# Sliding-window attention with a SwiGLU block: half of the first tile's shifted values by DMA, earlier keys for tile 1, and the last output rows in two column halves

## The chip, the cores and the metric

The kernel runs on one core of one Trainium2 chip. The metric is the device time of one execution in microseconds (us): 337.42 us is the median of three runs before the change (337.41 to 337.79). The profile is of one execution with a span of 335.7 us; times inside it count from the start of that span. Engine names are those of the profile: PE is TensorE (matmuls; PEld are its weight loads), DVE is VectorE, ACT is ScalarE, POOL is GpSimd, SP is SyncE. ACTq, SPq and POOLq are the engines' issues of transfers.

## What is computed

Eight batches of 8 heads with 576 positions and 64 channels go through causal attention with a window of 64 positions; the heads are joined, and each of the 4608 rows of 512 channels goes through a SwiGLU block of width 1536.

```python
scores = scale * np.matmul(q, k.transpose(0, 1, 3, 2))
mask = (rel >= 0) & (rel < window)                       # rel = query position - key position
attn = softmax(np.where(mask, scores, -1e9))
x = np.matmul(attn, v).transpose(0, 2, 1, 3).reshape(B * S, H * D)
g = x @ w_gate
out = (g * sigmoid(g) * (x @ w_val)) @ w_out
```

Inputs and output are float32 in HBM; the kernel multiplies in bfloat16 and accumulates in float32.

## The kernel before

The rows are worked in nine tiles of 512. A tile is 512 positions of one batch; tile 7 (LAST) gathers the last 64 positions of all eight. The order of the instructions on every engine is written out by hand: each engine takes its instructions in program order, and waits in order.

**A tile** has three stages. In the first, for each of four head pairs u, `scores` (L201) multiplies keys and queries into PSUM, ScalarE takes the exponential (L233) and VectorE the mask (L235). `sums` adds up the weights with a matmul by ones (`totals`, L245), and ScalarE makes the reciprocal from Ln and Exp (L253, L256). `values` (L265) multiplies the weights with v, block by block of 64 positions: even blocks take their values from `v2`, odd blocks from `v1`. `v2` holds the same values as `v1`, shifted by 64 positions (`shift_v`, L150: the lower half of a block's partitions comes from the block before, the upper half is copied). VectorE scales the product into xT (L277). In the second stage, `gate_value` (L302) runs for twelve values of m: four matmuls into a gate bank and four into a value bank, ScalarE's Silu (L299), and VectorE's product into hT (L300). Each bank has two buffers. In the third stage, `project` (L339) multiplies four groups of 128 rows with wo, twelve matmuls each over c (L315), VectorE copies the result from PSUM (L322), and four transfers of 32 rows store it (L334). The projection of tile t-1 is interleaved with the attention of tile t.

**Tile 0 and the opening** are written out by hand (L351 to L485). q, k and half of v of tile 0 come by transfers of SyncE and ScalarE, the other half of v by GpSimd's (L430), which cast on the way. TensorE runs matmuls on a tile of ones without use (`keep_warm`, L366) while it has nothing to do; their number in each place is fixed. GpSimd then issues in one row the gate weights (L442 to L447), the queries of tile 1 (`load_qk(1)`), wo in three parts (L449 to L451) and v of tile 1. They go through one queue in that order. GpSimd's issues have a limited number of lanes, and each waits for an earlier load in its lane. VectorE fills v2 of tile 0 in four copies (L462, L463, lines L155 and L156 of `shift_v`), after the last key split of tile 0 (L177). Then TensorE runs six warm matmuls, values of pairs 0 and 1, totals of pair 2 (`log_of`), gate matmuls, and totals of pair 3 between them.

**Keys of tile 1** come as float32 by four ScalarE transfers, issued in the gate loop of tile 0 at m = 3 to 6 (L500), are cast and joined by ScalarE at m = 7 to 10 (L505), transposed by TensorE and split by VectorE at m = 8 to 11 (L506 to L510). VectorE turns the queries of tile 1 at m = 10, 11 and twice after the loop (`turn_q`, L186). Then come scores(1,0) and scores(1,1), half of two projections of tile 0 with wo's parts c = 0 to 5, scores of the other two pairs, and c = 6 to 11.

**The end**: after the gates of tile 8, L582 runs four projections with nothing else left. Their stores are issued by SyncE and ScalarE in turn.

Of the kernel before, what the change touches and what calls it, by code (L numbers as in the profile page):

```python
# [8 lines left out]
P = 128  # L9
FP32 = mybir.dt.float32  # L10
# [7 lines left out]
def kernel(  # L18
# [10 lines left out]
    nc = tc.nc  # L29
    S, D, H = 576, 64, 8  # L30
    NTOK, DFF, DM = 4608, 1536, 512
    NT = NTOK // 512
# [9 lines left out]
    fsb = ctx.enter_context(tc.tile_pool(name="fsb", bufs=3))  # L42
# [6 lines left out]
    wo = cst.tile([P, 12, DM], BF16, name="wo")  # L49
# [4 lines left out]
    ones = cst.tile([P, 512], BF16, name="ones")  # L54
# [15 lines left out]
    staged, queries, weights, inverse, xT, hT = {}, {}, {}, {}, {}, {}  # L70

    def load_runs(eng, dst, src, t, hs):
        eng.dma_start(
            dst.rearrange("r h e d -> r h (e d)"),
            src[batch(t), hs, 0:512].rearrange("h (r e) d -> r h (e d)", e=4),
        )
# [73 lines left out]
    def shift_v(t, copy, lo=0, hi=4):  # L150

        a, b = v1[t % 2], v2[t % 2]
        top = min(hi, 3)
        if top > lo:
            copy(b[64:128, lo + 1:top + 1], a[64:128, lo:top])  # L155
        copy(b[0:64, lo:hi], a[0:64, lo:hi])  # L156
# [14 lines left out]
    def transposes(tp, src):  # L171

        for e in range(4):
            nc.tensor.transpose(tp[:, P * e:P * e + P], src[:, e], identb[:])  # L174
# [7 lines left out]
    def turn_q(t, u):  # L182

        if u == 0:
            queries[t] = att.tile([P, 4, 512], BF16, name="qT", tag="qT")
        nc.vector.transpose(  # L186
            queries[t][:, u, :].rearrange("r (e x) -> r e x", e=16),
            staged[t][0][:, u].rearrange("r (e d) -> r e d", d=D)[:, :, 0:32],
        )
# [53 lines left out]
    def totals(t, u, d_ps):  # L243
        for h in range(2):
            nc.tensor.matmul(  # L245
                d_ps[64 * h:64 * h + 64], ones[:, 0:D], weights[t, u][:, h, :]
            )

    def room(n):
        return fsb.tile([P, 2, 512], FP32, name="r", tag="r", bufs=4)[:, 0:n]  # L250

    def log(r, d_ps):
        nc.scalar.activation(r, d_ps, AF.Ln)  # L253
# [11 lines left out]
    def values(t, u, o_ps):  # L265
        E = weights.pop((t, u))
        if u == 0:
            xT[t] = att.tile([P, 4, 512], BF16, name="xT", tag="xT")
        for m in range(8):
            for h in range(2):  # L270
                nc.tensor.matmul(  # L271
                    blocks(o_ps[64 * h:64 * h + 64], t, m, m + 1),
                    (v1, v2)[m // 4][t % 2][:, m % 4, 2 * u + h, :] if t == LAST
                    else (v2, v1)[m % 2][t % 2][:, m // 2, 2 * u + h, :],
                    blocks(E[:, h, :], t, m, m + 1),
                )
        nc.vector.tensor_mul(xT[t][:, u, :], o_ps[:], inverse.pop((t, u)))  # L277
# [5 lines left out]
    def gate_part(t, ms, tiles, c):  # L283
        for m, pair in zip(ms, tiles):
            for ps, w in zip(pair, (wg, wv)):
                nc.tensor.matmul(  # L286
                    ps[:], w[:, c, P * m:P * m + P], xT[t][:, c, :],
                    start=(c == 0), stop=(c == 3),
                )

    def gate_tiles():
        return [ps_f.tile([P, 512], FP32, name=x + "_ps", tag=x) for x in "gv"]

    def gate_end(t, m, pair):
        if m == 0:
            hT[t] = hpool.tile([P, 12, 512], BF16, name="hT", tag="hT")
        g_ps, v_ps = pair
        sg = fsb.tile([P, 512], FP32, name="sg", tag="sg")
        nc.scalar.activation(sg[:], g_ps[:], AF.Silu)  # L299
        nc.vector.tensor_mul(hT[t][:, m, :], sg[:], v_ps[:])  # L300

    def gate_value(t, m):  # L302
        pair = gate_tiles()
        for ps, w in zip(pair, (wg, wv)):
            for c in range(4):
                nc.tensor.matmul(  # L306
                    ps[:], w[:, c, P * m:P * m + P], xT[t][:, c, :],
                    start=(c == 0), stop=(c == 3),
                )
        gate_end(t, m, pair)  # L310

    def project_part(t, ss, tiles, cs):
        for c in cs:
            for s, o_ps in zip(ss, tiles):
                nc.tensor.matmul(  # L315
                    o_ps[:], hT[t][:, c, P * s:P * s + P], wo[:, c, :],
                    start=(c == 0), stop=(c == 11),
                )

    def project_end(t, s, o_ps):  # L320
        os_ = fsb.tile([P, 512], FP32, name="os_", tag="os_", bufs=3)
        nc.vector.tensor_copy(os_[:], o_ps[:])  # L322
        rows = out[S * batch(t):S * batch(t) + 512]
        if t < TURNED:
            nc.sync.dma_start(rows.rearrange("(r e) f -> e r f", e=4)[s], os_[:])
            return
        if t == LAST:
            rows = out.rearrange("(b s) f -> b s f", s=S)[:, 512:S]
            rows = rows.rearrange("b (r e) f -> e b r f", e=16)
        else:  # L330
            rows = rows.rearrange("(r e) f -> e r f", e=16)
        for i in range(4):
            eng = nc.scalar if t == NT - 1 and i % 2 else nc.sync
            eng.dma_start(rows[4 * s + i], os_[32 * i:32 * i + 32])  # L334

    def out_tile():
        return ps_f.tile([P, 512], FP32, name="o_ps", tag="g")

    def project(t, s):  # L339
        o_ps = out_tile()  # L340
        project_part(t, (s,), (o_ps,), range(12))
        project_end(t, s, o_ps)

    def set_exp():
        nc.scalar.preload_act_table_set("natural_log_exp_and_others")

# [6 lines left out]
    for u in range(4):  # L353
        hs = slice(2 * u, 2 * u + 2)
# [1 line left out]
        load_runs(nc.scalar if u < 2 else nc.sync, raw[1][:, hs], k, 0, hs)  # L356
    load_v(nc.sync, staged[0, "v"], 0, (0, 1))
    set_exp()
    nc.vector.memset(ones[:], 1.0)
    make_identity(nc, identb[:])  # L360
    nc.vector.memset(zero[:], 0.0)
    for i in range(2):
# [1 line left out]
    warm = ps_f.tile([P, 512], FP32, name="warm", tag="v")  # L364

    def keep_warm(n):  # L366
        for _ in range(n):
            nc.tensor.matmul(warm[0:D], ones[:, 0:D], ones[:])

    keep_warm(7)  # L370
    nc.gpsimd.memset(tri[:], 1.0)
    for a in range(2):
        half = tri[64 * a:64 * a + 64]
        nc.gpsimd.affine_select(
            out=half[:, 1 - a], in_=half[:, 1 - a], compare_op=ALU.is_ge, fill=0.0,
# [3 lines left out]
            out=half[:, a], in_=half[:, a], compare_op=ALU.is_ge, fill=0.0,  # L379
# [19 lines left out]
    on_v, on_p, on_a = nc.vector.tensor_copy, nc.gpsimd.tensor_copy, nc.scalar.copy  # L399
# [4 lines left out]
    def wide(name):  # L404
        return ps_a.tile([P, 2, 512], FP32, name=name, tag="a")

    def join(copy, dst, src):
        copy(dst.rearrange("r e (h d) -> r h e d", h=2), src)

    def one(name):  # L410
        return ps_a.tile([P, 2, 512], FP32, name=name, tag="a")[:, 0]
# [43 lines left out]
    d_ps, r = wide("d_ps"), room(2)  # L455
# [4 lines left out]
    invert(r)  # L460
    scores(0, 3)
    shift_v(0, on_v, 0, 2)  # L462
    shift_v(0, on_v, 2, 4)  # L463

    def log_of(u):
        d_ps = one("d_ps")
        totals(0, u, d_ps)
        inverse[0, u] = room(1)[:, 0]
        log(inverse[0, u], d_ps)

    keep_warm(6)
    for u in range(2):
        values(0, u, ps_f.tile([P, 512], FP32, name="ao_ps", tag="gv"[u])[:])
    log_of(2)
    pairs = [gate_tiles() for _ in range(2)]
    gate_part(0, (0,), pairs, 0)
    log_of(3)
    gate_part(0, (1,), pairs[1:], 0)
    for u in (2, 3):
        invert(inverse[0, u])  # L480
    values(0, 2, one("ao_ps"))
# [6 lines left out]
    for m in range(12):  # L488
        if m < 2:
            gate_end(0, m, pairs[m])  # L490
        else:
            gate_value(0, m)
        if m == 2:
            for i in range(4):
                nc.vector.tensor_copy(
                    mask[:, 0, :, i], tri[:].rearrange("r c (x e) -> r e c x", e=16)
                )
            nc.vector.memset(mask[64:128, 0, :, 0, 0, :], 0.0)
            nc.vector.tensor_copy(mask[:, 1], mask[:, 0])
        if 3 <= m < 7:  # L500
            hs = slice(2 * m - 6, 2 * m - 4)
            load_runs(nc.scalar, raw_k[:, hs], k, 1, hs)
        if 7 <= m < 11:
            u = m - 7
            join(on_a, keys[:, u], raw_k[:, 2 * u:2 * u + 2])  # L505
        if m >= 8:  # L506
            u = m - 8
            tp = ps_a.tile([P, 512], BF16, name="tp", tag="a")
            transposes(tp, keys[:, u])
            split_k(kT[1][:, u, :], tp[:])  # L510
        if m >= 10:
            turn_q(1, m - 10)
    turn_q(1, 2)
    turn_q(1, 3)

    set_exp()
# [27 lines left out]
    for t in range(1, NT):  # L544
# [31 lines left out]
        for m in range(12):  # L576
# [2 lines left out]
                turn(t + 1, turns.index(m))  # L579
            if m == 8 and 3 <= t < 7:  # L580
                turn_k(kT[2], k_l, t - 3)
    for s in range(4):  # L582
        project(NT - 1, s)

# [1 line left out]
_INS = ['q', 'k', 'v', 'moe_w_gate', 'moe_w_val', 'moe_w_out']  # L586
# [26 lines left out]
```

The softmax here doesn't subtract the row's maximum and nothing guards it: scores larger than these inputs give would overflow.

## Time and profile before

| what | us |
|---|---|
| time, median of 3 | 337.42 |
| span of the profile | 335.7 |
| PE busy | 323.2 (96%) |
| DVE busy | 214.2 (64%) |
| ACT busy | 169.2 (50%) |
| POOL busy | 137.8 (41%) |
| gate matmuls L306, g and v | 107.6 and 108.3 |
| projection matmuls L315 | 96.5 |
| gate loop of tile 0 on PE | 21.29 to 39.6 |
| last matmul of the projection to the end of the span | 331.2 to 335.7 |

The page is one execution: busy time per engine, the chain of work that ended last followed back from the last instruction, and groups of instructions with their busy time, the mean duration of one, and the idle time ahead of them with what ended it. A wait for several things is put down to the one that came last. A line of the timeline begins with start and length in us, then engine, line, operation and tile; a bracket at its end holds the engine's idle time before it and the releaser.

### The profile page before, as it was taken

The numbers are of one execution on the slowest core, as the hardware profiler recorded it, in microseconds if no ns is written. First come the engines' busy times: TensorE is split into PE (matmuls) and PEld (weight loads), VectorE is DVE, ScalarE is ACT, GpSimd is POOL, SyncE is SP. The second block draws the span as 40 slices with busy tenths as digits, with TensorE's granted clock in tenths as the row PEclk, the third lists the DMA queues.
The fourth block names the chain that finished last, engine by engine and source line by source line (L and its number), as shares of the span: only waits on it lengthen the run. The fifth ranks groups of instructions, "written<-read, shape, count | busy, mean of one in ns | idle before, by whom it ended". The sixth has DMA issues, their size and how long they took to land.

```text
span 335.7 us, 6932 instructions
## 1 busy us (share of the span) xinstructions
PE 323.2 (96%) x2683; PEld 153.9 (46%) x2729; DVE 214.2 (64%) x318; ACT 169.2 (50%) x241; POOL 137.8 (41%) x247
## 2 busy tenths in 40 slices
PE   8899799999999999999999999999999999999994
PEld 3444344444544454445444544444444444544441
DVE  5754766588667756785678656865786476753431
ACT  4764656336733763366435553565347633763300
POOL 5944345946767965256123896163200000000000
PEclk9999999999999999999999999999999999999999
DMA  7999999999899499639931999199401320010013
GB/s 261 205 202 226 229 188 223 125 205 215 147 248 186 52 176 234 124 58 209 185 89 20 170 180 167 12 189 177 111 0 48 79 56 3 23 72 31 3 32 94
DMA packets 83057, 44.12 MB, mean 131 GB/s; under 512 B 63824, under 2 KB 77648, under 8 KB 83024
## 3 DMA queue, kind: packets, MB, share of 16 engines
q0 software_dynamic: 49328, 22.56, 54.2%
q1 hardware_dynamic: 31680, 19.02, 20.6%
q10 hardware_dynamic: 2016, 2.10, 2.2%
q8 instruction: 21, 0.34, 0.4%
q14 instruction: 12, 0.10, 0.1%
HBM read 54.00 MB, written 9.44 MB: 189 GB/s over the span
## 4 chain that ended last, share of the span: by engine, by line
PE 88%; DMA 6%; DVE 3%; issue 2%; ACT 1%; DVEq 0%
PE g_ps L306 26%; PE v_ps L306 26%; PE o_ps L315 25%; PE s_ps L227 3%; DMA k_f<-in_k_dram 3%; PE ao_ps L271 3%; PE d_ps L245 3%; DMA q_f<-in_q_dram 1%; PE tp L174 1%; PE g_ps L286 1%; ACT E L233 1%; DVE kT L177 1%; PE v_ps L286 1%; DMA out_dram<-os__4409 1%; DMA out_dram<-os__4428 1%
## 5 line engine op out<-in xcount | busy, mean ns | idle before, releaser
L299 ACT ACTIVATE sg<-g_ps 128x512 f32<-128x512 f32 x108 | 64.4, 597 | 112.1 <-PE g_ps L306 79.9
L300 DVE TENSOR_TENSOR hT<-sg,v_ps 128x512 bf16<-128x512 f32 x108 | 74.9, 694 | 62.9 <-PE v_ps L306 59.9
L306 PE MATMUL v_ps<-xT,wv 128*128 128x512 bf16 x417 | 108.3, 379 | 0.5
L306 PE MATMUL g_ps<-xT,wg 128*128 128x512 bf16 x413 | 107.6, 379 | 0.5
L315 PE MATMUL o_ps<-wo,hT 128*128 128x512 bf16 x405 | 96.5, 380 | 1.6 <-issue 0.6
L107 POOL DMA_DIRECT2D k_s<-in_k_dram x112 | 60.7, 551 | 29.8 <-DMA q_s<-in_q_dram 20.5
L306 PEld LDWEIGHTS <-wv 128*128 128x128 bf16 x424 | 41.5, 98 | 50.0
L306 PEld LDWEIGHTS <-wg 128*128 128x128 bf16 x424 | 41.4, 98 | 49.5 <-issue 0.3
L315 PEld LDWEIGHTS <-hT 128*128 128x128 bf16 x432 | 39.6, 98 | 45.1 <-issue 0.4
L233 ACT ACTIVATE E<-s_ps 128x1024 bf16<-128x1024 f32 x36 | 35.2, 1021 | 8.4 <-PE s_ps L227 8.2
L277 DVE TENSOR_TENSOR xT<-ao_ps,r 128x512 bf16<-128x512 f32 x36 | 24.7, 691 | 22.7 <-ACT r L256 20.5
L196 DVE STREAM_TRANSPOSE kT<-k_s 128x512 bf16<-128x512 bf16 x28 | 35.9, 1284 | 0.0
L253 ACT ACTIVATE r<-d_ps 128x512 f32<-128x512 f32 (+1 forms) x35 | 21.0, 601 | 22.4 <-PE d_ps L245 22.4
L235 DVE TENSOR_TENSOR E<-E,mask 128x1024 bf16<-128x1024 bf16 x28 | 20.5, 739 | 11.5 <-ACT E L233 11.5
L87 POOL DMA_DIRECT2D q_s<-in_q_dram x28 | 15.3, 558 | 26.7 <-DVE qT L186 16.0
L148 POOL CAST v<-v_f 128x512 bf16<-128x512 f32 x22 | 14.3, 665 | 21.5 <-DMA v_f<-in_v_dram 17.5
L256 ACT ACTIVATE r<-r 128x512 f32<-128x512 f32 (+1 forms) x35 | 22.3, 641 | 1.1
L186 DVE STREAM_TRANSPOSE qT<-q_s 128x512 bf16<-128x512 bf16 x32 | 22.3, 702 | 0.0
L271 PEld LDWEIGHTS <-v 128*64 128x64 bf16 x576 | 13.8, 112 | 5.7 <-issue 1.7
L271 PE MATMUL ao_ps<-E,v 128*64 128x64 bf16 x576 | 15.3, 196 | 0.6 <-DVE v L156 0.6
L245 PE MATMUL d_ps<-E,ones 128*64 128x512 bf16 x72 | 13.9, 392 | 0.3
L227 PE MATMUL s_ps<-qT,kT 64*64 64x128 bf16 (+1 forms) x640 | 12.5, 211 | 0.2 <-DVE kT L177 0.2
(95 smaller groups left out, 175.6 us busy)
## 6 DMA issues: line engine op xcount, KB each, us to landing
q_s<-in_q_dram POOLq DMA_DIRECT2D x28, 248.0 KB, 6.7
k_s<-in_k_dram POOLq DMA_DIRECT2D x112, 56.0 KB, 5.2
v_f<-in_v_dram SPq DMA_DIRECT2D x22, 256.0 KB
v<-in_v_dram POOLq DMA_DIRECT2D x18, 128.0 KB, 4.8
k_f<-in_k_dram ACTq DMA_DIRECT2D x6, 256.0 KB
wo<-in_moe_w_out_dram POOLq DMA_DIRECT2D x3, 512.0 KB, 16.0
v<-v SPq DMA_DIRECT2D x6, 256.0 KB
v<-v SPq DMA_DIRECT2D x6, 192.0 KB
```

The lines of the kernel that those rows point to most:

```text
L107: nc.gpsimd.dma_start(k_s[p0:p0 + 32, g, :, 0:w], k[b, a:H:2, s:s + P].rearrange("u (r e) d -> r u (e d)", e=4) [:, :, 32 * c:32 * c + w],)
L186: nc.vector.transpose(queries[t][:, u, :].rearrange("r (e x) -> r e x", e=16), staged[t][0][:, u].rearrange("r (e d) -> r e d", d=D)[:, :, ...
L196: nc.vector.transpose(dst[:, u, :].rearrange("r (g x e) -> r g e x", g=4, e=4), k_s[:, :, u].rearrange("r g (e d) -> r g e d", d=D)[:, :, ...
L227: nc.tensor.matmul(blocks(s_ps[64 * c:64 * c + 64, h], t, lo, hi), zero[r] if src is None else src[r, u, x:x + 64], blocks(qT[r], t, lo, h ...
L233: nc.scalar.activation(E[:], s_ps[:], AF.Exp, scale=0.125)
L245: nc.tensor.matmul(d_ps[64 * h:64 * h + 64], ones[:, 0:D], weights[t, u][:, h, :])
L271: nc.tensor.matmul(blocks(o_ps[64 * h:64 * h + 64], t, m, m + 1), (v1, v2)[m // 4][t % 2][:, m % 4, 2 * u + h, :] if t == LAST else (v2, v ...
L277: nc.vector.tensor_mul(xT[t][:, u, :], o_ps[:], inverse.pop((t, u)))
L299: nc.scalar.activation(sg[:], g_ps[:], AF.Silu)
L300: nc.vector.tensor_mul(hT[t][:, m, :], sg[:], v_ps[:])
L306: nc.tensor.matmul(ps[:], w[:, c, P * m:P * m + P], xT[t][:, c, :], start=(c == 0), stop=(c == 3),)
L315: nc.tensor.matmul(o_ps[:], hT[t][:, c, P * s:P * s + P], wo[:, c, :], start=(c == 0), stop=(c == 11),)
```

## The change

Four things are done.

1. The shifted values: of the four copies that fill v2 of tile 0, the last two (blocks 2 and 3) go from VectorE to two SyncE transfers inside SBUF. The order on TensorE changes with it: five warm matmuls in place of six, totals of pair 2 before values of pairs 0 and 1, totals of pair 3 directly after them, and then the gate matmuls of m = 0 and 1 together.
2. Keys of tile 1: loads at m = 1 to 4, casts at m = 5 to 8, transposes at m = 6 to 9, each two iterations sooner; the query turns are at m = 9, 10 and 11 and once after the loop, each one sooner.
3. The warm-up at the start: the tile of ones is filled in two parts, and TensorE starts with six matmuls of 128 columns on the first part, and then six of 512 in place of seven.
4. The last group of 128 rows (s = 3 of tile 8) is projected in two halves of 256 columns, in a bank each. Each half is copied and stored on its own, with four transfers of 32 rows of 256 columns.

It is for a shorter start, keys of tile 1 that are there when they are wanted, and a shorter end.

```diff
+    def project_last(t, s):
+        rows = out[S * batch(t):S * batch(t) + 512].rearrange("(r e) f -> e r f", e=16)
+        os_ = fsb.tile([P, 512], FP32, name="os_", tag="os_", bufs=3)
+        tiles = out_tile(), out_tile()
+        for x in range(2):
+            f = slice(256 * x, 256 * x + 256)
+            for c in range(12):
+                nc.tensor.matmul(
+                    tiles[x][:, 0:256], hT[t][:, c, P * s:P * s + P], wo[:, c, f],
+                    start=(c == 0), stop=(c == 11),
+                )
+            nc.vector.tensor_copy(os_[:, f], tiles[x][:, 0:256])
+            for i in range(4):
+                eng = nc.scalar if i % 2 else nc.sync
+                eng.dma_start(rows[4 * s + i][:, f], os_[32 * i:32 * i + 32, f])
...
-    nc.vector.memset(ones[:], 1.0)
+    nc.vector.memset(ones[:, 0:P], 1.0)
+    nc.vector.memset(ones[:, P:512], 1.0)
...
-    keep_warm(7)
+    for _ in range(6):
+        nc.tensor.matmul(warm[0:D, 0:P], ones[:, 0:D], ones[:, 0:P])
+    keep_warm(6)
...
     shift_v(0, on_v, 0, 2)
-    shift_v(0, on_v, 2, 4)
+    shift_v(0, shift_dma, 2, 4)
...
-    keep_warm(6)
+    keep_warm(5)
+    log_of(2)
     for u in range(2):
         values(0, u, ps_f.tile([P, 512], FP32, name="ao_ps", tag="gv"[u])[:])
-    log_of(2)
+    log_of(3)
     pairs = [gate_tiles() for _ in range(2)]
-    gate_part(0, (0,), pairs, 0)
-    log_of(3)
-    gate_part(0, (1,), pairs[1:], 0)
+    gate_part(0, (0, 1), pairs, 0)
...
-        if 3 <= m < 7:
-            hs = slice(2 * m - 6, 2 * m - 4)
+        if 1 <= m < 5:
+            hs = slice(2 * m - 2, 2 * m)
             load_runs(nc.scalar, raw_k[:, hs], k, 1, hs)
-        if 7 <= m < 11:
-            u = m - 7
+        if 5 <= m < 9:
+            u = m - 5
             join(on_a, keys[:, u], raw_k[:, 2 * u:2 * u + 2])
-        if m >= 8:
-            u = m - 8
+        if 6 <= m < 10:
+            u = m - 6
             tp = ps_a.tile([P, 512], BF16, name="tp", tag="a")
             transposes(tp, keys[:, u])
             split_k(kT[1][:, u, :], tp[:])
-        if m >= 10:
-            turn_q(1, m - 10)
-    turn_q(1, 2)
+        if m >= 9:
+            turn_q(1, m - 9)
     turn_q(1, 3)
...
-    for s in range(4):
+    for s in range(3):
         project(NT - 1, s)
+    project_last(NT - 1, 3)
```

## The prediction

> **What bounds the kernel now.** I read the page's chain of work first, then TensorE's waits, then the chain and the timeline of the first 49 us and the last 16 us. The page:
>
> ```profile
> PE 88%; DMA 6%; DVE 3%; issue 2%; ACT 1%; DVEq 0%
> ```
>
> TensorE is the bound: busy 323.2 of 335.7 us. A gain must come from the few places where it isn't fed, or from the ends. TensorE's waits list them:
>
> ```profile
> PE s_ps L227 <- DVE qT L186: 1.7, 1, 1.7
> PE ao_ps L271 <- DVE v L156: 0.6, 1, 0.6
> PE g_ps L286 <- DVE xT L277: 0.4, 1, 0.4
> ```
>
> After 50 us TensorE waits for nothing but 0.6 us of issue. The first wait (42.02 us, scores of tile 1) is the largest; the chain says what stands behind it (start, length, what):
>
> ```profile
> 29.26 9.63 DMA k_f<-in_k_dram
> ...
> 39.44 0.60 ACT sg L299
> ...
> 40.66 0.68 DVE kT L177
> 41.35 0.63 DVE qT L186
> ...
> 42.02 0.42 PE s_ps L227 x18
> 42.45 0.54 PE o_ps L315 x2
> ```
>
> The last key load of tile 1 lands at 38.9, its cast holds back the last sg, that holds back hT, and behind hT the key split and the query turns queue on VectorE. In the timeline, the first key load and the last wo load, then the end:
>
> ```profile
> 24.08 0.37 ACTq L73 DMA_DIRECT2D k_f<-in_k_dram  x1
> ...
> 31.74 0.62 ACT L408 CAST k_b<-k_f 128x512 bf16<-128x512 f32 x1 [0.16 <-DMA k_f<-in_k_dram]
> ...
> 45.06 0.54 POOL L87 DMA_DIRECT2D q_s<-in_q_dram  x1 [1.96 <-DMA v<-in_v_dram]
> ...
> 331.26 0.69 DVE L322 COPY os__4447<-o_ps 128x512 f32<-128x512 f32 x1 [1.90 <-DMA out_dram<-os__4428]
> 331.98 0.78 SPq L334 DMA_DIRECT2D out_dram<-os__4447  x2
> ```
>
> A key load takes 7.7 us from issue to use. The DMA view of 24.0 to 27.8 us shows only the software queue moving, though three key loads were issued in it:
>
> ```profile
> q0 software_dynamic: 1244, 0.76, 137.7%
> ```
>
> So a transfer issued by ScalarE or SyncE while GpSimd's queue is deep starts nearly 4 us late. This decides the new shift transfers.
>
> [...]
>
> **The opening, up to tile 0's gates.** Four copies fill v2 in chain: 12.37 to 14.94. The last two (0.58, 0.43) go; two SyncE transfers of 64 and 128 KB replace them. They wait for v1's blocks 2 and 3, loads issued at 6.33 with 4.8 us at best to landing: about 11.4 and 12.3. TensorE's order becomes: warm x5, totals of pair 2, values(0,0). Warm starts at 12.73; 5 x 0.2155 + 2 x 0.2155 ends at 14.24; values of blocks 0 and 1 need only the first two copies (13.88) and end by 14.4. Then TensorE waits for the transfers, and all gates are queued behind it. This new wait is in no trace. Lower bound: q_f with empty queues took 3.3 us (0.82 to 4.11), so 15.6 for the second. Upper bound: the key load's 7.7 us, a larger one: about 20. I take 4.1 us, the late start just seen being a little shorter when only two or three 256 KB loads are ahead, and 192 KB being small: L = 16.4.
>
> From L on: rest of values(0,0) 0.33, xT 0.70 on VectorE with values(0,1) and the totals of pair 3 below it, ending about L+1.15; four gate matmuls to L+2.0, values 0.37 to L+2.4, four gates to L+3.25, values to L+3.6, xT(3) hidden by the four c=2 gates, c=3 to L+5.35. ScalarE's logs are no longer between: pair 2's log starts at 15.11, after the last exp. Gate loop start = L+5.35 = 21.75, against 21.29 before: this part loses 0.45 us. Without the wait it would win 1.4.
>
> **The key loads two iterations sooner.** The loop has 80 matmuls: 17.25 us, plus four transpose groups of about 0.23 us inside it (three before). It ends at L+5.35+17.25+0.9 = L+23.5 = 39.9. The loads go out after sg 1 to 4, from 22.2; at 7.7 us for the first and about 2.2 to 2.9 for each next (before: 31.7, 34.7, 36.8, 38.9) they reach ScalarE at 29.5 to 36.5, cast right behind sg 5 to 8. A late cast delays the next sg by at most some 1.3 us, and gate banks have two buffers of 1.72 us of matmuls: hidden. The casts' transposes stand at m=6 to 9. The query turns, 0.70 each, follow hT 9, 10, 11. q_s must be there: its last queue wait in GpSimd ends at 37.26 and VectorE used it at 39.18; earlier key packets push it by about 0.7 us and the shifts by 0.5, so 37 to 38.4; the first turn is due at 37.5. Both first turns end by 39.9, scores(1,0) and (1,1) run without a break to L+24.3 = 40.7. Before: 42.44. So this path gains 18.14 - L = 1.74 us; the saved wait of 1.66 is most of it.
>
> But next is the projection that reads wo. GpSimd saw wo's parts land by 39.98, 42.55 and 45.06 (each wait for a lane is put to wo, the last to v, which queues behind it). The third is first read at c=8, before at 45.66+4 x 0.2155 = 46.5. These loads are bandwidth-bound and the shifts put about 0.5 us ahead of them. Landing lies between 44.5 (allowing 0.5 for GpSimd's reaction) and 45.06, so 45.0 to 45.6: gain capped at 0.9 to 1.5. I take 1.25 us.
>
> From there TensorE is unbroken to the end in before, so the gain is carried; tile 2's turns (65.80) follow loads whose issue ended at 60.2, and don't bind.
>
> **Warm-up.** Splitting the ones memset (0.48) lets TensorE start some 0.3 us earlier, with six short matmuls in place of a seventh long one (7 in 3.20 us); the first data come at 4.79 anyway. [...] the shifts' landing hangs on GpSimd's loads: 0.
>
> **The end.** The last rows take 24 matmuls of 256 columns: 24 x 0.109 = 2.62 against 2.59, +0.03, if the 98 ns weight loads stay hidden under 109 ns. They did under shorter ones: L271 has 16 pairs in 0.37, L174 4 in 0.36. The first half's copy and stores lie under the second half's 1.3 us. The last copy has 256 columns: [...] saves 0.27. The last stores carry 1 KB rows, not 2: about -0.1. Their four issues per queue, 0.4 each, are done in time: two at 330.4, two at 331.7. Sum: -0.35 us. Bounds: -0.5, and +2.0 if no weight load were hidden (24 x 0.207).
>
> Sum: -1.25 - 0.35 = -1.6, so 337.42 - 1.6 = 335.8 us.
>
> **Rivals.**
> (a) Late shifts: L = 17.6, with the start delay of the key load in full for the second transfer. Gain 18.14 - 17.6 = 0.5, with the end 0.9: 336.5. For it: key loads' 7.7. [...]
> (b) wo or q_s sets the pace: the opening's earlier work only waits for the same bytes, since the DMA engines are busy throughout 11 to 52 us. Gain 0.1 + 0.3: 337.0, no change. For it: the share of DMA, 9 tenths in nearly every slice. Against: 1.5 us between 45.06 and 46.5.
> (c) The shifts take the key load's whole 7.3 to 7.7 us: L = 19.6. 18.14 - 19.6 = -1.5, end +0.35: 338.5, slower. So does a tail with bare weight loads: 337.42 - 1.25 + 2.0 = 338.2. For it: a wait where VectorE had an in-order sure finish at 14.94. Against: it takes until L > 18.5 to lose.
>
> **Chances.** As forecast 0.60; (a) 0.20, of which a quarter falls within 0.2% (above 336.75); (b) 0.10; (c) 0.10. Faster 0.60 + 0.15 = 0.75, same 0.05 + 0.10 = 0.15, slower 0.10. The range runs from the best bounds (cap 1.5, end 0.5[...]: 335.2) to just past (b), 337.1.
>
> **What would show it.** TensorE's waits: ao_ps waiting for DMA v<-v about 2 us instead of 0.6 for VectorE; the wait for qT gone; gate loop starting near 21.75; scores(1,1) ending near 40.7; perhaps a short wait of o_ps for wo. At the end a 0.42 us copy near the same distance from the last matmul. Wrong if the wait for v<-v exceeds 4 us, if qT still waits (for q_s instead of keys), or if the 256-column matmuls are spaced over 0.12 us.

## The result, and the profile after

The changed kernel takes 340.03 us (median of four runs, 339.56 to 340.46), the kernel before 337.61 us; the ratio is 1.007 with a 95% interval of 1.0053 to 1.0088. The change makes the kernel slower by 2.4 us, where 1.6 us less was forecast. Runs of one kernel differ in clock: 26 of the 83 runs of the kernel before that stand beside the experiments have a mean granted clock of 0.992 to 0.994 and take about 1.5 us longer than the rest, and of the changed kernel's four runs two have 0.989 (340.07 and 340.46 us), where the profiled one, the fastest, has 0.994. The profiled execution has a span of 337.5 us (335.7 before).

The line numbers of the changed kernel differ a little from those of before: the shift transfers are L421, the last projection is L351, warm matmuls are L385 and L388, casts of q and k are L427.

The shares of the page's chain of work hardly moved, and TensorE is as busy as before (323.9 us):

```profile
PE 88%; DMA 7%; issue 1%; ACT 1%; DVE 1%; POOL 0%; SPq 0%; DVEq 0%; POOLq 0%
```

TensorE's waits in the changed kernel (engine, line, what ended the wait: us in total, times, longest) show what became of the waits of before:

```profile
PE ao_ps L271 <- DMA v<-v: 3.7, 1, 3.7
PE g_ps L286 <- DVE xT L277: 0.4, 1, 0.4
```

The wait of 1.7 us for qT before scores(1,1) is gone, as meant. In place of the 0.6 us for VectorE's copy stands one of 3.7 us for the new transfers. The chain of the first 60 us in order of time (start, length, what):

```profile
12.70 5.42 DMA v<-v
...
18.15 0.33 PE ao_ps L271 x8
...
19.33 0.58 PE g_ps L286
19.92 0.43 PE v_ps L286
20.34 0.43 PE g_ps L286
20.77 0.43 PE v_ps L286
...
25.46 1.02 PE g_ps L306 x4
...
44.55 0.59 PE s_ps L227 x34
45.14 0.54 PE o_ps L315 x2
```

There are two things to see. TensorE resumes at 18.15; before, it was at 14.99:

```profile
14.99 0.57 PE L271 MATMUL ao_ps<-E,v 128*64 128x64 bf16 x24 [0.65 <-DVE v L156]
```

And the gate matmuls behind it are 0.43 us apart, double the 0.2155 us of before: TensorE's clock has fallen (0.50 in the second stretch below). By 23 us they take 0.22 us again. The busy times by stretch (the stretch and its length; then busy time and instructions of PE, PEld, DVE, ACT and POOL; then the granted clock, the DMA engines' mean busy share and GB/s) put bounds to that:

```profile
15.00:19.20 4.20, 0.79 (x26) 0.58 (x27) 0.61 (x2) 0.93 (x3) 3.43 (x5) 1.00 1.41 212
19.20:22.60 3.40, 2.94 (x22) 1.26 (x23) 1.37 (x3) 2.70 (x4) 1.58 (x3) 0.50 1.33 205
22.60:30.00 7.40, 7.36 (x49) 3.24 (x48) 4.42 (x11) 2.31 (x5) 2.31 (x4) 1.00 1.29 208
```

TensorE is busy 0.79 of 4.20 us, and then runs for 3.4 us at clock 0.50. The timeline shows the issue of the two transfers, the first key load, a cast of keys that waits for its load and the transposes of TensorE right behind it, the start of the last projections, and the copies at the end:

```profile
11.86 1.33 SPq L421 DMA_DIRECT2D v<-v  x2
...
25.25 0.37 ACTq L73 DMA_DIRECT2D k_f<-in_k_dram  x1
...
35.68 0.62 ACT L427 CAST k_b<-k_f 128x512 bf16<-128x512 f32 x1 [1.66 <-DMA k_f<-in_k_dram]
...
36.36 0.40 PE L174 MATMUL tp<-identb,k_b 128*128 128x128 bf16 x4 [0.15 <-ACT k_b L427]
...
323.39 7.93 PE L315 MATMUL o_ps<-wo,hT 128*128 128x512 bf16 x36
...
332.67 0.42 DVE L355 COPY os__4439<-o_ps 128x256 f32<-128x256 f32 x1 [0.62 <-PE o_ps L351]
...
333.98 0.43 DVE L355 COPY os__4439<-o_ps 128x256 f32<-128x256 f32 x1 [0.89 <-PE o_ps L351]
```

The same start of the last projections, in the kernel before:

```profile
320.70 10.52 PE L315 MATMUL o_ps<-wo,hT 128*128 128x512 bf16 x47
```

The span adds up: the projection after scores(1,1) starts at 45.07 instead of 42.38 (in the chains, 45.14 and 42.45), so the first 45 us lose 2.7 us. From the first matmul of the last projections (323.39; before 320.70) to the end of the span it takes 14.1 us instead of 15.0: the end wins 0.9. Together 1.8 us, the difference of the spans.

### The profile page after: what moved, and what is told of

Read it like the earlier page. It is cut to its first block, busy times and chain, and to the rows that moved or that the text cites. A ratio compares the mean times of both kernels' runs of the same rounds, so it can differ in the third digit from the quotient of the medians.

```text
span 337.5 us, 6976 instructions
## 1 busy us (share of the span) xinstructions
PE 323.9 (96%) x2700; PEld 155.3 (46%) x2745; DVE 213.2 (63%) x318; ACT 169.0 (50%) x241; POOL 137.7 (41%) x247
## 4 chain that ended last, share of the span: by engine, by line
PE 88%; DMA 7%; issue 1%; ACT 1%; DVE 1%; POOL 0%; SPq 0%; DVEq 0%; POOLq 0%
PE o_ps L315 26%; PE g_ps L306 26%; PE v_ps L306 26%; DMA k_f<-in_k_dram 3%; PE ao_ps L271 3%; PE s_ps L227 3%; PE d_ps L245 3%; DMA v<-v 2%; DMA v<-in_v_dram 1%; DMA q_f<-in_q_dram 1%; PE o_ps L351 1%; PE v_ps L286 1%; PE g_ps L286 1%; ACT E L233 1%; POOL v L128 0%
## 5 line engine op out<-in xcount | busy, mean ns | idle before, releaser
L315 PE MATMUL o_ps<-wo,hT 128*128 128x512 bf16 x394 | 94.0, 380 | 1.6 <-issue 0.6
L315 PEld LDWEIGHTS <-hT 128*128 128x128 bf16 x420 | 38.4, 98 | 43.7 <-issue 0.4
L271 PEld LDWEIGHTS <-v 128*64 128x64 bf16 x576 | 14.1, 113 | 9.2 <-DMA v<-v 3.8
```

What stands on the lines that cost most here:

```text
L271: nc.tensor.matmul(blocks(o_ps[64 * h:64 * h + 64], t, m, m + 1), (v1, v2)[m // 4][t % 2][:, m % 4, 2 * u + h, :] if t == LAST else (v2, v ...
L315: nc.tensor.matmul(o_ps[:], hT[t][:, c, P * s:P * s + P], wo[:, c, :], start=(c == 0), stop=(c == 11),)
```

## The experiments

My theory after this result: the two transfers start late behind GpSimd's queue, and the wait for them costs twice, as a wait and by the half speed that follows; the other parts win about what was forecast. The rival: the new order and the earlier keys are what costs, by fuller transfer queues.

**The transfers alone**, in the kernel before:

```diff
-    shift_v(0, on_v, 2, 4)
+    shift_v(0, shift_dma, 2, 4)
```

> The kernel before, with only the last two shift copies made transfers of SyncE. Theory: values(0,0) resumes at about 18 us instead of 14.99 and the clock falls for one stretch of about 3.4 us: 341 to 342.5. Rival (the transfers are as good as hidden and something else costs): 337.6 to 339.

Measured: 341.82 us against 337.68 of before, ratio 1.0124 (1.0093 to 1.0155). TensorE's waits of this kernel:

```profile
PE ao_ps L271 <- DMA v<-v: 3.9, 1, 3.9
...
PE s_ps L227 <- DVE qT L186: 1.5, 1, 1.5
```

values(0,0) resumes at 18.10, and the chain has gate matmuls 0.43 us apart until 25.31:

```profile
18.10 0.33 PE ao_ps L271 x8
...
19.86 0.43 PE v_ps L286
...
25.31 0.39 PE v_ps L286
25.70 0.22 PE g_ps L286
...
27.03 1.02 PE g_ps L306 x4
```

The part alone costs 4.1 us between the medians: the theory. But one thing was not expected: the half speed lasts from 18.70 to 25.51 us here, 6.8 us and not 3.4. The profiled execution is the slowest of the four, 342.82 us at a mean clock of 0.988; two of the others have 0.994 and 0.995 and take 341.4 and 341.3 us, which fits one stretch of 3.4 us (the changed kernel's profiled execution, with one, has 0.994), but they were not traced.

**Everything but the transfers**: the changed kernel with the copies back.

```diff
-    shift_v(0, shift_dma, 2, 4)
+    shift_v(0, on_v, 2, 4)
```

> The changed kernel, with the two SyncE transfers put back to VectorE copies and nothing else undone. Theory (the transfers land about 3 us after the copies would have ended, and TensorE's clock falls in the wait; the other parts win): the wait of ao_ps on v<-v is gone, the gate loop of tile 0 starts at 20.3 to 21.2 us instead of 25.5, no half-speed stretch, time 335.0 to 336.2. Rival (the new order on TensorE and the earlier keys are what costs, through fuller transfer queues): the time stays above 338.5.

Measured: 335.46 us, ratio to before 0.9932 (0.9909 to 0.9956); the mean granted clock is 1.0. This one line is worth 4.6 us against the changed kernel and makes a kernel faster than both. The gate loop starts at 20.32. The rival is out: order, keys, end and warm-up together win 2.2 us. TensorE's waits in it name the next limit, and the timeline shows where the two waits for wo stand:

```profile
PE o_ps L315 <- DMA wo<-in_moe_w_out_dram: 0.9, 2, 0.7
PE s_ps L227 <- DVE qT L186: 0.4, 1, 0.4
```

```profile
42.35 1.02 PE L315 MATMUL o_ps<-wo,hT 128*128 128x512 bf16 x4 [0.67 <-DMA wo<-in_moe_w_out_dram]
...
45.14 1.89 PE L315 MATMUL o_ps<-wo,hT 128*128 128x512 bf16 x7 [0.21 <-DMA wo<-in_moe_w_out_dram]
```

The longer one is for wo's second part (c = 4), the shorter for its last (c = 8).

**The clock**: the changed kernel with warm matmuls where TensorE would stand idle.

```diff
     keep_warm(5)
     log_of(2)
+    keep_warm(14)
```

> The changed kernel with 14 more warm matmuls (some 3 us) between the totals of pair 2 and values(0,0), where TensorE would stand idle for the transfers. Theory (half of the loss is the wait itself, and some 1.6 us of it is TensorE's half speed from 19.2 to 22.6 us that follows the idle time): the transfers land as late (about 18.1), but there is no half-speed stretch: 338.1 to 338.9. Rival (the clock follows something else, or costs nothing on the path): 339.6 to 340.4.

Measured: 337.81 us, ratio to before 1.0001 (0.9982 to 1.0019). Fourteen matmuls without use win 2.2 us of the changed kernel's 340.03; I had expected 1.1 to 1.9. The timeline shows that TensorE still waits for the transfers at their landing, now for only 0.36 us, and then when the gate loop and the projection start:

```profile
17.48 0.57 PE L271 MATMUL ao_ps<-E,v 128*64 128x64 bf16 x24 [0.36 <-DMA v<-v]
...
23.33 1.02 PE L306 MATMUL g_ps<-xT,wg 128*128 128x512 bf16 x4
...
42.26 2.76 PE L315 MATMUL o_ps<-wo,hT 128*128 128x512 bf16 x11
```

and the stretches show full clock after it:

```profile
15.00:19.20 4.20, 3.45 (x47) 1.93 (x46) 1.29 (x2) 1.26 (x3) 3.17 (x6) 1.00 1.42 212
19.20:22.60 3.40, 3.24 (x44) 1.57 (x43) 1.39 (x3) 2.02 (x3) 1.57 (x3) 1.00 1.31 205
```

This execution is one of the faster of twelve (336.78 us), so it is compared with the changed kernel's profiled one and not with the medians. From TensorE's resumption to the gate loop it takes 5.85 us (17.48 to 23.33), as in the run with the new order alone further down (14.84 to 20.69), against 7.31 in the changed kernel (18.15 to 25.46): the half speed costs 1.5 us there. The projection starts 2.8 us sooner (42.26 against 45.07); 0.7 of the rest is an earlier landing, of which 0.3 is the issue (11.53), and 0.7 is a shorter gate loop (18.93 against 19.61). So the clock is about half of what the fill shows, not all of it. The wait itself remains: this kernel is 2.35 us behind the one with the copies.

**Why they land late**: GpSimd does a cast of v and six memsets on a scratch tile before it issues the first gate weights, so its queue is almost empty when the transfers are issued.

```diff
-    weights_gv(0, 256)
     cast_v(0, (0, 1))
+    for _ in range(6):
+        nc.gpsimd.memset(idle[:], 0.0)
+    weights_gv(0, 256)
```

> The changed kernel with GpSimd busy for some 6 us of memsets (of a scratch tile) before it issues the first gate weights, so that its queue is empty when the two SyncE transfers are issued. Only their time to landing is asked; the whole gets slower since the weights come late. Theory (they start late behind the queued weight loads): TensorE resumes 2.3 to 3.3 us after the second issue, instead of 5.5 us. Rival (a transfer inside SBUF of 64 rows is slow in itself): still 5 us or more.

The timeline of this kernel has the issues and TensorE's resumption:

```profile
11.60 1.30 SPq L422 DMA_DIRECT2D v<-v  x2
...
14.68 0.57 PE L272 MATMUL ao_ps<-E,v 128*64 128x64 bf16 x24 [0.48 <-DMA v<-v]
```

From the first issue to use it takes 3.1 us, against 6.3 in the changed kernel (11.86 to 18.15); from the second issue, some 0.8 us later, 2.3 against 5.4. The DMA view of 11.6 to 14.6 us of this kernel (GB/s in 40 equal slices; then packets, MB, time as a share of 16 engines) has the SyncE queue's 0.20 MB in it:

```profile
GB/s 73 55 44 22 9 10 9 0 0 0 0 0 0 0 0 0 123 232 218 178 82 41 0 0 0 0 218 218 300 137 300 137 246 137 28 28 0 0 0 0
q1 hardware_dynamic: 160, 0.20, 28.3%
q0 software_dynamic: 138, 0.02, 8.9%
```

That of 11.86 to 14.0 us of the changed kernel has of the two queues only the software one:

```profile
q0 software_dynamic: 898, 0.40, 147.4%
```

and that of 12.7 to 17.2 us has both, the SyncE queue (q1) from 14.0 on:

```profile
q0 software_dynamic: 1547, 0.77, 128.7%
q1 hardware_dynamic: 159, 0.20, 12.6%
```

So the same transfers are quick where hardly anything is queued. Behind GpSimd's loads the first of their packets moves 2.1 us after the issue; but with the software queue empty it is also 1.2 us (12.8), so the late start is only 0.9 of the 3.2 us between the two kernels. The larger part comes after it: from the first packet to the last it takes about 3.3 us (14.0 to 17.3) against 1.6 (12.8 to 14.4), with the software queue's packets between, and from the last packet to TensorE's use 0.8 against 0.3. The whole of this kernel took 344.74 us in its one run, since the weights came late: TensorE waited 6.1 and 2.6 us for wg and wv.

**The other parts, one at a time**, each in the kernel before. The earlier keys and turns (the lines of the loop in the diff, nothing else):

```diff
-        if 3 <= m < 7:
-            hs = slice(2 * m - 6, 2 * m - 4)
+        if 1 <= m < 5:
+            hs = slice(2 * m - 2, 2 * m)
...
-        if m >= 10:
-            turn_q(1, m - 10)
-    turn_q(1, 2)
+        if m >= 9:
+            turn_q(1, m - 9)
```

> The kernel before, with only the keys of tile 1 loaded, cast and transposed two iterations sooner and the query turns one sooner. Theory: the wait of 1.7 us on qT before scores(1,1) goes; wo's landing may cap it: 336.0 to 336.4. Rival (wo or the queries set the pace, nothing is won): 337.3 to 337.7, with a new wait of PE on wo or qT.

Measured: 336.36 us, ratio 0.9947 (0.9931 to 0.9964): 1.3 us won between the medians. The ratio is worth 1.8 us: it takes in all runs, and none of this kernel's 14 has the lower clock that 13 of the 33 runs of before beside it have. TensorE's wait on qT is gone and one on wo has come:

```profile
PE o_ps L315 <- DMA wo<-in_moe_w_out_dram: 0.8, 2, 0.6
```

The new order in the opening:

```diff
-    keep_warm(6)
+    keep_warm(5)
+    log_of(2)
     for u in range(2):
         values(0, u, ps_f.tile([P, 512], FP32, name="ao_ps", tag="gv"[u])[:])
-    log_of(2)
+    log_of(3)
     pairs = [gate_tiles() for _ in range(2)]
-    gate_part(0, (0,), pairs, 0)
-    log_of(3)
-    gate_part(0, (1,), pairs[1:], 0)
+    gate_part(0, (0, 1), pairs, 0)
```

> The kernel before, with only the new order on TensorE in the opening (five warm matmuls, totals of pair 2 first, totals of pair 3 after the values of pair 1, all gates of the first quarter together). Theory: the gate loop starts 0.8 to 1.0 us sooner (20.3 to 20.5), and since the key loads are issued from the loop they come sooner too: 336.6 to 337.1. Rival (totals ahead of the values only shift the same work): 337.5 to 337.8.

Measured: 336.95 us against 337.64, ratio 0.9972 (0.9958 to 0.9985): 0.7 us won; the gate loop starts at 20.69 instead of 21.29, 0.6 us sooner and not the 0.8 to 1.0 expected.

The end:

```diff
-    for s in range(4):
+    for s in range(3):
         project(NT - 1, s)
+    project_last(NT - 1, 3)
```

> The kernel before, with only the last 128 rows in two column halves. By the forecast's sum 0.35 us less (337.2); by the changed kernel's trace up to 0.9 us less (336.7). Rival (weight loads not hidden under 256 columns): 338 or more.

Measured: 336.91 us, ratio 0.9975 (0.9961 to 0.9988): 0.8 us won.

The warm-up:

```diff
-    keep_warm(7)
+    for _ in range(6):
+        nc.tensor.matmul(warm[0:D, 0:P], ones[:, 0:D], ones[:, 0:P])
+    keep_warm(6)
```

(with ones filled in two parts, as in the change)

> The kernel before, with only the warm-up at the start changed (ones filled in two parts, six short matmuls and six of 512 in place of seven). Forecast's price 0: 337.4 to 337.8. Rival ([...] the opening gains): 336.8 to 337.2.

Measured: 337.52 us against 337.67, ratio 0.9993 (0.9976 to 1.001): no difference that can be told from none. A gain of some tenths is not ruled out either: the first eight transposes take 0.62 to 1.03 us in the traces, and short and long ones occur both with the old warm-up and with the new one.

**What caps the sum**: alone the four win 1.3 + 0.7 + 0.8 + 0.15 = 2.95 us, together (copies back) 2.2. So I put the old order on TensorE back into the kernel with the copies back (the diff of the order above, reversed).

> The changed kernel with the copies back on VectorE and with the old order on TensorE in the opening, so that only the earlier keys, the end and the warm-up are new. Theory (wo's last part caps what the opening can win, so the new order's 0.7 us is not added to the keys' 1.3 us): 335.4 to 335.8, as with the new order. Rival (the gains add up): 336.0 to 336.4.

Measured: 335.40 us, ratio 0.9933 (0.9911 to 0.9954), the same as with the new order. TensorE's waits of this kernel, and the place of the one for wo:

```profile
PE o_ps L315 <- DMA wo<-in_moe_w_out_dram: 0.7, 1, 0.7
```

```profile
42.55 1.02 PE L315 MATMUL o_ps<-wo,hT 128*128 128x512 bf16 x4 [0.67 <-DMA wo<-in_moe_w_out_dram]
```

With the keys early, the order wins nothing more: the cap is wo, as expected, but the wait is for its second part and not for its last. Could the wait for wo be filled? In the kernel with the copies back, the sums of pairs 0 and 1 of tile 1 were put ahead of the second half of that projection:

```diff
-        if u % 2:
-            project_part(0, (0, 1), halves, range(3 * u - 3, 3 * u + 3))
+        if u == 1:
+            project_part(0, (0, 1), halves, range(6))
...
     for u in range(2):
         sums(1, u, d_tile())
+    project_part(0, (0, 1), halves, range(6, 12))
+    for s in range(2):
+        project_end(0, s, halves[s])
```

(with the copies, loads and shifts that followed the projection moved along)

> The changed kernel with the copies back on VectorE, and the sums of pairs 0 and 1 of tile 1 moved ahead of the second half of the projection that waited 0.9 us for wo. Theory (wo's last part sets the pace there): the wait for wo goes or shrinks to under 0.2 us, 334.6 to 335.0. Rival (the sums wait for their masks, or the time comes back in the next wait): 335.3 to 335.6, as with the copies back alone.

Measured: 335.78 us, ratio 0.9941 (0.9922 to 0.996): nothing won. TensorE's waits say where it went:

```profile
PE s_ps L227 <- DVE qT L186: 0.6, 1, 0.6
PE o_ps L315 <- DVE os__770 L322: 0.6, 1, 0.6
...
PE o_ps L315 <- DMA wo<-in_moe_w_out_dram: 0.4, 1, 0.4
```

The expectation had the place wrong. The longer of the two waits for wo, 0.67 us at c = 4, lies in the first half of the projection, ahead of the moved sums, and they could fill only the shorter one, 0.21 us at c = 8, which is gone. The 0.4 us that stays is at c = 4 (42.56 us); it is shorter since this projection starts 0.5 us later (40.30 against 39.78), after a longer wait for qT. And the next projection waits for the copy that frees its bank, which now follows at once. Whether work put ahead of c = 4 would win something is not tested.

## Why the prediction was wrong

The step that failed is the price of the new wait: 4.1 us from the second transfer's issue to its landing, which gave L = 16.4. It took 5.45 us, and L was 18.15. A second step is missing from the sum: the fall of TensorE's clock behind the wait, to 0.50 for 3.4 us. Together with two smaller errors they make up the first 45 us:

| stretch on TensorE | forecast, us | profiled execution, us | too long by |
|---|---|---|---|
| resumption, L | 16.4 | 18.15 | 1.75 |
| from L to the gate loop, at full clock | 5.35 | 5.85 (warm fill, order alone) | 0.5 |
| the half clock in it | none | 1.46 | 1.5 |
| gate loop to the projection | 18.95 | 19.61 | 0.7 |
| the projection starts | 40.7 | 45.07 | 4.4 |

- **The landing.** Of the 1.75 us, 0.4 are the second issue, which waits for v's block and came at 12.70 and not at 12.3. The other 1.35 are the transfer, whose 5.45 us lie in the middle of the bounds that had been written down (3.3 and 7.7). The start behind GpSimd's queue was read rightly from the key load of before; that the packets would also take twice as long from first to last, 3.3 us against 1.6, was not priced. By the prediction's own formula the path gain is 18.14 - 18.15 = 0: at this landing the change's opening would have won nothing, and with the end's gain the kernel would still have been a little faster.
- **The sum behind it.** 5.85 us against 5.35, at full clock: the groups of matmuls have gaps of about 0.1 to 0.2 us between them, which were put at nothing.
- **The clock.** No term of the sum had it. The gate loop should have started 5.85 us after L, at 24.0, and started at 25.46; the 1.46 us between are the stretch at half speed. The trace has a wait of 3.7 us and then 3.4 us at clock 0.50 (19.16 to 22.58); in the 3.4 us just ahead of the fall TensorE was busy for 0.79. With the gap filled by warm matmuls, and a wait of 0.36 us left, the clock is 1.00 from 19.20 to 22.60. Whether the wait of 2 us that was forecast would have kept the clock no run shows. The record makes it doubtful: where the trace has the wait of 1.7 us for qT (the kernel before, and the runs with the order, the end or the warm-up alone), 34 of 135 runs have the lower mean clock, and where it is gone or under 0.7 us and no long wait has taken its place, none of 42. The lower clock, 0.993 against 0.998, is by an estimate what one stretch of 3.4 us at half speed gives (half of 3.4 in some 336 us is 0.005), but none of these 34 runs was traced, so this is not shown.
- **The loop after it.** A late key cast was priced as hidden. It was not: three of the four casts waited 1.0 to 1.7 us for their loads, and the transposes on TensorE that follow them started at 36.36, 38.50 and 40.70, each 0.05 us after its cast had ended and 0.2 to 0.3 us after the gate matmuls ahead of it. That is the 0.7 us. With the warm fill, where the transposes hardly wait, the stretch took 18.93 us, as worked out.
- **Right**: keys and turns. The wait on qT goes, the gain is capped by wo, and 1.25 us were forecast; 1.3 measured in the key run, where the wait for wo's last part ends at 45.50, within the 45.0 to 45.6 forecast. The cap itself is shown by the runs with the old and the new order, which give the same time. What the forecast overlooked is wo's second part: with the copies back it holds TensorE longer (0.67 us) than the last. With the copies back, all of the opening wins some 1.4 us (2.2 less the end's 0.8).
- **Right in kind, too large**: the order without the wait. 1.4 us were forecast for the gate loop's start if nothing is waited for; with the order alone, where the copies end at 14.78, it was 0.6 (20.69), and 1.0 with everything but the transfers (20.32). The 0.5 us of gaps above are most of the difference.
- **Right in kind, small in size**: the end. -0.35 was forecast, -0.8 measured. The copy took 0.43 instead of 0.69, as priced, and the weight loads of the 24 matmuls were hidden as priced: the matmuls of 256 columns start 0.109 us apart, with weight loads of 98 ns (the first matmul to the last copy's start is 10.59 us against 10.56). The stores' term was mis-sized: from the end of the last copy to the end of the span it is 3.1 us against 3.75, -0.65 and not -0.1 (-0.55 in the run with the end alone). The stores carry half the bytes; why it is worth that much no run separates. No trace of before showed the price of 0.42 for the copy; measured are 678 to 693 ns for 512 float columns (L322) and, in the changed kernel, 0.42 and 0.43 us for 256 (L355), more than half of it.
- **Right**: the warm-up, priced 0, is within the noise.
- None of the rivals came true as written. For the landing (a) is nearest, with L = 17.6; for the outcome it is (c), which had the kernel slower, but from L = 19.6, which did not come: 18.15, the clock and the late casts together did what 19.6 alone would have done, and more.

## What to carry to other kernels

A transfer that replaces a compute copy must be priced from a transfer that was issued into the same queues at the same time, from issue to use, and not from bytes: here 192 KB took 6.3 us beside another queue's loads and 3.1 us without them, and only 0.9 of the difference was a later start. When a change adds a wait to TensorE, look at the granted clock behind it as well as at the wait: here 3.4 us at clock 0.50 followed a wait of 3.7 us and cost 1.5 us, and fourteen useless matmuls in the gap got that back. And when several edits go in together, run each alone: one line of this change hid a gain of 2.2 us.

## What was not expected of the hardware

- With GpSimd's loads queued, the DMA engines moved no packet of a SyncE transfer for 2.1 us after its issue at 11.86; with the software queue empty the first packet still came only after 1.2 us. Once both queues moved, the 0.20 MB took about 3.3 us from first packet to last, against 1.6.
- A wait of 3.7 us on TensorE was followed by 3.4 us at clock 0.50 that began about 1 us after the work had resumed. With the transfers alone a wait of 3.9 us was followed by 6.8 us at half speed, with TensorE busy for 3.1 of the first 3.4.
- Two half-sized last stores instead of one full one end the span 0.55 to 0.65 us sooner after the last copy, with the copy's own gain of 0.26 not counted.
